# FNet mixing with a gated GLU on one core: the first tile of x cut in halves and shared by three DFT chunks

## The chip, the core and the metric

The program runs on one core of one Trainium2 chip. The core has five engines with a queue each: TensorE (matrix multiply, PE in the profile; its weight loads are PEld), VectorE (DVE), ScalarE (ACT), GpSimd (POOL) and SyncE (SP), which here only issues loads from device memory. An engine works through its own queue in order; a semaphore holds an instruction until what it reads has been written. The metric is the device time of one execution in microseconds (us), median of several runs; lower is better.

## The reference, cut to what matters

```python
x = A_x                                  # [1, 2048, 512], float32
xn = _layernorm(x, axis=-1)              # (x - mean) / sqrt(var + 1e-5)
a = einsum("bsd,ed->bse", xn, dft_hid_re)
b = einsum("bsd,ed->bse", xn, dft_hid_im)
s = einsum("ts,bse->bte", dft_seq_re, a) - einsum("ts,bse->bte", dft_seq_im, b)
g = silu(einsum("bsf,fd->bsd", sigmoid(xn @ w_gate) * (xn @ w_up), w_down))
return x + s * g
```

The sequence has 2048 rows, the hidden width is 512, the GLU's inner width 1792. The DFT matrices and weights are inputs like any other.

## The kernel before, in words

All matrix products are made in a fast 32-bit form that rounds its operands. To keep the accuracy each operand is cut into a high part (the rounded value) and a low part (value minus high part), and each product is made of three matmuls: high by high, low by high, high by low (`mm3`, line 68). The high part is a copy on ScalarE that rounds as it writes (L120, L375), the low part a subtraction on VectorE (L125, L378). The products are arranged in Strassen's manner (seven products for eight), which is why sums of blocks are made on the way.

The program is one list of **units**, written out by hand in order. A unit is a small group of matmuls. Before unit n is issued, loads for the units up to n + 5 are issued, operands of the units up to n + 2 are cut in parts, and functions hung on n run: `sooner(n, ...)` before that cutting, `amid(n, ...)` after it and before the unit's matmuls, `after(n, ...)` behind them. As each engine works in order, this list sets the order on every queue.

The first stage is the DFT along the sequence. x lies in four row tiles for each half j of the sequence, `xs[j, pp]`, each of 2 x 512 columns on 128 partitions (index e = 0, 1 for the two rows that a partition holds). The DFT matrix comes in chunks t of 512 columns; the first three chunks run together (`TOGETHER = 3`). Units 0, 1, 2 are tile 0 of x with chunks 0, 1, 2; units 3, 4, 5 are tile 1; units 6, 7, 8 are tile 2; units 9 to 11 tile 3. Each such unit has 12 matmuls (two column blocks d, two halves e, three part products). The weights of the matmul are the parts of normalised x, the moving operand the parts of the chunk.

A tile of x needs its layer norm first. `stats` (L165) runs on VectorE the statistics of a row (L178) and their aggregate (L179) and adds epsilon (L171); GpSimd makes minus the mean (L172), the power -1/2 (L173) and the bias (L174). ScalarE then writes the normalised high part, and normalises x in place (`normed`, L372); VectorE makes the low part (L378). For the first tile `begin` does this by hand with every load, high part and low part in its place; `settle` (L449) normalises x in place on VectorE. While nothing has landed, TensorE runs 13 matmuls on a tile of ones, whose results are not used.

For tile 1, `begin` makes parts too. For tiles 2 and 3 `begin_seq` hangs them on the units: statistics four units ahead, high part of the chunk and `prepare` two units ahead.

Tile pages of 4 KB on each partition come from one pool of 54; loads go down SyncE's queue in program order.

Of the kernel before, what the change touches and what calls it, by code (L numbers as in the profile page):

```python
# [8 lines left out]
F32 = mybir.dt.float32  # L9
# [23 lines left out]
def fnet_glu_kernel(ctx: ExitStack, tc: tile.TileContext, x, x_t, c_re, c_im, w_h, w_gu, w_down, out):  # L33
# [14 lines left out]

    ones = const.tile([P, 512], F32R, name="ones")
    nc.vector.memset(ones.bitcast(F32), 1.0)  # L50
# [103 lines left out]
    def fetch(j, pp):  # L154
        xs[j, pp] = page([2, D], F32)
        if (j, pp) == (0, 0):
            for e in range(2):
                nc.sync.dma_start(xs[j, pp][:, e, :], halves(x[pp, j])[:, e, :])
        else:
            nc.sync.dma_start(xs[j, pp], x[pp, j])  # L160

    def moment(pp, m, j):
        return moments[:, pp, m, j, :]

    def stats(j, pp, apart=False):  # L165
        mv = stat.tile([P, 2, 2], F32, name="mv")
        rs = stat.tile([P, 2], F32, name="rs")

        def scale(e):
            mean, by, bias = (moment(pp, m, j)[:, e] for m in range(3))  # L170
            nc.vector.tensor_scalar(rs[:, e], mv[:, e, 1], EPS, None, op0=ALU.add)  # L171
            nc.gpsimd.tensor_tensor(mean, mv[:, e, 0], minus[:, e], op=ALU.mult)  # L172
            nc.gpsimd.tensor_tensor(by, rs[:, e], mhalf[:, e], op=ALU.pow)  # L173
            nc.gpsimd.tensor_tensor(bias, mean, by, op=ALU.mult)  # L174

        for e in range(2):
            st = stat.tile([P, 6], F32, name="st")
            nc.vector.bn_stats(st, xs[j, pp][:, e, :])  # L178
            nc.vector.bn_aggr(mv[:, e, :], st)  # L179
# [44 lines left out]

    def c_block(t, pp, j, m):
        v = (c_re, c_im)[m][j, pp, t]
        return Load(halves(v) if t < 2 and pp == j == m == 0 else v, [2, SB])

    class Sum(Value):
# [22 lines left out]

    TOGETHER = 3
    CHAIN = {1: "a", 6: "a", 7: "a", 4: "a", 2: "b", 5: "c", 3: "c"}

    class Chunk:
# [33 lines left out]

        def run(self, k, pp):
            ch = "p" if k < 3 and self.t < TOGETHER else CHAIN[k]
            if k in (1, 5) and pp == 0:
# [85 lines left out]

    def prepare(pp):  # L380
        parts, src = tile_of(pp)
        for e in range(2):
            normed(pp, parts[0], src, e)
        for e in range(2):
            normed(pp, src, src, e)
        return parts, src

    def begin_seq():
        tags = {"p": "a", "c": "pd", "a": "a"}, {"p": "b", "c": "b", "a": "c"}, {"p": "c", "c": "pd", "a": "a"}, {"a": "c", "b": "a", "c": "pd"}
        chunks = [Chunk(t, tags[t], t in (1, 2)) for t in range(NT)]  # L390
        for i, k in enumerate((1, 2)):
            for pp in range(4):
                for c in chunks[:TOGETHER]:
                    add(c.needs(k, pp), lambda c=c, k=k, pp=pp: c.run(k, pp))
                m = TOGETHER * (4 * i + pp)
# [4 lines left out]
                else:  # L400
                    if pp > 1:
                        sooner(m - 4, lambda pp=pp: stats(0, pp, True))
                        sooner(m - 2, units[m][0][1].high)
                        sooner(m - 2, lambda pp=pp: ready.append(prepare(pp)))
                        for e in range(2):
                            amid(m - 2, lambda e=e: low(*ready[-1], e))
                    if pp > 2:
# [18 lines left out]
    def begin(chunks):  # L426
        for i, tag in enumerate(("gb", "ub", "pd", "pd")):
            idle = bank(tag)
            for _ in range((4, 4, 3, 2)[i]):
                nc.tensor.matmul(idle, ones[:, :P], ones, start=True, stop=True)  # L430
        first, second = (chunks[t].op[1, 0] for t in range(2))
        fetch(0, 0)
        for c in (first, second):
            c.raw = c.loads[0].at = page([2, SB], F32)
            c.parts = page([2, SB]), page([2, SB])
            for e in range(2):
                nc.sync.dma_start(c.raw[:, e, :], c.loads[0].src[:, e, :])
        fetch(0, 1)
        for n in (2, 3):
            units[n][0][1].load()  # L440
        fetch(0, 2)
        for n in (4, 5):
            units[n][0][1].load()
        mv = stats(0, 0, True)
        a, src = tile_of(0)

        def settle(e):
            v = src[:, e]
            nc.vector.tensor_scalar(v, v, mv[:, e, 0:1], moment(0, 1, 0)[:, e : e + 1], op0=SUB, op1=ALU.mult)  # L449

        normed(0, a[0], src, 0)
        for e in range(2):
            high(first.parts, first.raw, e)
        settle(0)
        low(a, src, 0)
        settle(1)
        high(a, src, 1)
        for e in range(2):
            low(first.parts, first.raw, e)
        low(a, src, 1)  # L460
        first.at = first.parts
        for e in range(2):
            high(second.parts, second.raw, e)
        second.get()
        units[2][0][1].high()
        stats(0, 1, True)
        a, src = tile_of(1)
        normed(1, a[0], src, 0)
        normed(1, src, src, 0)
        units[2][0][1].get()  # L470
        low(a, src, 0)
        units[3][0][1].high()
        normed(1, a[0], src, 1)
        normed(1, src, src, 1)
        units[3][0][1].get()
        low(a, src, 1)

# [479 lines left out]
def _layout(inputs):  # L957
# [25 lines left out]
    c_re = seq(inputs["A_dft_seq_re"])  # L983
    apart([x[0, 0], c_re[0, 0, 0], c_re[0, 0, 1]])
    return {
# [26 lines left out]
```

## Time and profile before

| | |
|---|---|
| median of 3 runs | 793.86 us (793.84 to 794.58) |
| the profiled execution | 793.51 us, of which the span of the profile is 791.7 us |
| granted TensorE clock in that execution | 0.999 of full speed |
| TensorE matmuls | 3469, busy 786.4 us |
| VectorE, ScalarE, GpSimd busy | 670.9, 518.9, 142.6 us |
| moved by DMA | 182.07 MB, mean 230 GB/s |
| DMA from 8 to 40 us of the span | above 400 GB/s, busy throughout |

A row of the timeline has the start in us, the length in us, engine, line of the kernel, operation, what is written and read, shape, how often in a row, and in brackets how long the engine had been idle before and what ended that. Instructions of one engine overlap a little at their ends, so the distance of two starts is shorter than a length. A row of a group has line, engine, operation, names and shapes, count, then busy us and mean ns of one, then idle time before them. A row of loads has destination and source, queue, count, size of one, and us from issue to landing. SPq is SyncE's queue.

### The profile page before, as it was taken

Reading aid. Unit: us, or ns where it says so; the run is one execution under the profiler, and the core shown is the slowest. Engines: PE = TensorE matmul, PEld = TensorE weight load, DVE = VectorE, ACT = ScalarE, POOL = GpSimd, SP = SyncE. Lnnn points to the kernel's source line nnn. Section 1 sums busy time; section 2 is a strip of 40 time slices with the busy share of each in tenths; the row PEclk is TensorE's granted clock in tenths of the full one; section 3 lists DMA queues with packets and bytes.
Section 4 is the critical chain, followed back from the end, with each engine's and each line's share of the span. In section 5 each row is a group of like instructions: output and inputs, shape, how many; then the busy total and the mean of one; then the engine's idle time right before and its main releaser. Section 6 shows DMA issues by size and latency. Waiting matters only on the chain.

```text
span 791.7 us, 9921 instructions
## 1 busy us (share of the span) xinstructions
PE 786.4 (99%) x3469; PEld 650.8 (82%) x3469; DVE 670.9 (85%) x879; ACT 518.9 (66%) x791; POOL 142.6 (18%) x198
## 2 busy tenths in 40 slices
PE   9999999999999999999999999999999999999998
PEld 7888888888888888888888888888888888888886
DVE  7887999788869798899999888668869898896967
ACT  6995755535434546677887867576577787887571
POOL 4452000000111002012111131122222111111301
PEclk9999999999999999999999999999999999999999
DMA  9949673385797246849965996799999898999996
GB/s 345 408 145 304 153 266 134 134 317 198 253 336 223 106 144 219 236 176 213 207 127 96 222 243 171 225 206 292 299 291 258 185 230 218 231 288 304 268 352 175
DMA packets 53186, 182.07 MB, mean 230 GB/s; under 512 B 5904, under 2 KB 6160, under 8 KB 53136
## 3 DMA queue, kind: packets, MB, share of 16 engines
q0 software_dynamic: 23360, 77.62, 44.4%
q1 hardware_dynamic: 29776, 103.82, 35.9%
q8 instruction: 27, 0.44, 0.2%
q14 instruction: 23, 0.19, 0.1%
HBM read 114.29 MB, written 70.27 MB: 233 GB/s over the span
## 4 chain that ended last, share of the span: by engine, by line
PE 99%; DMA 0%; DVE 0%; ACT 0%; POOL 0%; issue 0%; POOLq 0%
PE pd L72 28%; PE ga L72 17%; PE ua L72 17%; PE uc L72 12%; PE gc L72 12%; PE gb L72 7%; PE ub L72 7%; DMA page<-in_x_dram 0%; DVE st L178 0%; ACT page L372 0%; POOL moments L173 0%; ACT page L375 0%; DVE page L880 0%; DVE page L881 0%; POOL moments L174 0%
## 5 line engine op out<-in xcount | busy, mean ns | idle before, releaser
L125 DVE TENSOR_TENSOR page<-page 128x1024 fp32r<-128x1024 f32 (+1 forms) x381 | 346.6, 940 | 70.9 <-ACT page L120 69.2
L120 ACT ACTIVATE page<-page 128x512 fp32r<-128x512 f32 (+1 forms) x380 | 299.6, 830 | 113.7 <-DVE page L129 92.0
L72 PE MATMUL pd<-page 128*128 128x512 f32 (+1 forms) x972 | 236.9, 388 | 0.0
L72 PEld LDWEIGHTS pd<-page 128*128 128x128 f32 x972 | 182.0, 188 | 37.5
L129 DVE TENSOR_TENSOR page<-page 128x1024 f32<-128x1024 f32 (+2 forms) x244 | 195.4, 820 | 0.9
L72 PE MATMUL ga<-page 128*128 128x512 f32 x600 | 157.0, 389 | 0.2 <-ACT page L375 0.2
L72 PE MATMUL ua<-page 128*128 128x512 f32 x600 | 156.8, 389 | 0.0
L72 PEld LDWEIGHTS ga<-page 128*128 128x128 f32 x600 | 112.6, 188 | 24.4 <-ACT page L375 1.0
L72 PEld LDWEIGHTS ua<-page 128*128 128x128 f32 x600 | 112.6, 188 | 23.3
L556 POOL DMA_DIRECT2D g_part<-page x76 | 65.3, 859 | 266.4 <-ACT page L565 150.9
L72 PE MATMUL gc<-page 128*128 128x512 f32 x408 | 106.6, 389 | 0.0
L72 PE MATMUL uc<-page 128*128 128x512 f32 x408 | 106.6, 389 | 0.0
L565 ACT ACTIVATE page<-pd 128x512 f32<-128x512 f32 x140 | 82.4, 598 | 24.7 <-PE pd L72 17.4
L72 PEld LDWEIGHTS uc<-page 128*128 128x128 f32 x408 | 76.6, 188 | 15.9
L72 PEld LDWEIGHTS gc<-page 128*128 128x128 f32 x408 | 76.6, 188 | 15.9
L72 PE MATMUL gb<-page 128*128 128x512 f32 (+1 forms) x240 | 62.4, 383 | 0.0
L72 PE MATMUL ub<-page 128*128 128x512 f32 x228 | 60.9, 389 | 0.0
L72 PEld LDWEIGHTS gb<-page 128*128 128x128 f32 x240 | 44.2, 188 | 8.9
L72 PEld LDWEIGHTS ub<-page 128*128 128x128 f32 x228 | 42.8, 188 | 8.9
L314 POOL DMA_DIRECT2D f_raw<-page x16 | 8.8, 548 | 195.7 <-DVE page L326 134.8
L673 ACT ACTIVATE page<-ga 128x512 f32<-128x512 f32 x28 | 16.6, 593 | 17.9 <-PE ga L72 15.9
L691 DVE TENSOR_TENSOR page<-page 128x512 f32<-128x512 f32 x28 | 19.3, 689 | 10.0 <-ACT page L688 9.3
(101 smaller groups left out, 381.8 us busy)
## 6 DMA issues: line engine op xcount, KB each, us to landing
g_part<-page POOLq DMA_DIRECT2D x84, 512.0 KB, 7.2
page<-in_c_re_dram SPq DMA_DIRECT2D x46, 512.0 KB, 7.8
page<-in_c_im_dram SPq DMA_DIRECT2D x32, 512.0 KB, 6.8
page<-f_raw SPq DMA_DIRECT2D x28, 512.0 KB, 7.6
page<-in_w_gu_dram SPq DMA_DIRECT2D x22, 512.0 KB, 6.0
f_raw<-page POOLq DMA_DIRECT2D x16, 512.0 KB, 5.8
f_sum<-page POOLq DMA_DIRECT2D x16, 512.0 KB, 7.3
page<-f_sum SPq DMA_DIRECT2D x16, 512.0 KB, 10.2
```

Of the source, the lines that this page charges most:

```text
L72: nc.tensor.matmul(ps, ws[w], ms[m], start=first and i == 0, stop=last and i == 2, skip_group_check=go_on)
L120: nc.scalar.activation(self.parts[0], self.raw, AF.Copy)
L125: nc.vector.tensor_tensor(lo, self.raw, hi.bitcast(F32), op=SUB)
L129: (engine or nc.vector).tensor_tensor(dst, a, b, op=op)
L314: nc.gpsimd.dma_start(f_raw[self.t][block], v)
L556: nc.gpsimd.dma_start(g_part[i], pg, accum_op=ADD)
L565: nc.scalar.activation(pg[:, o, :], po, AF.Copy, scale=float(sign))
L673: nc.scalar.activation(s[k][:, m, :], ps[c + "a"], AF.Copy)
L691: nc.vector.tensor_mul(s[k][:, 0, :], s[k][:, 0, :], ps["u" + tag] if tag else s[k][:, 1, :])
```

## The change

- **Ones.** The warming matmuls read a broadcast constant of the framework instead of a tile that VectorE fills; there are 10 (3, 3, 2, 2) instead of 13.
- **Loads.** In host memory the first half (e = 0) of the first tile of x is laid out in two pieces of 256 columns, and the first block of the third chunk is laid out by halves like those of the first two. `begin` loads the two pieces, the first half of all three chunks, the second half of x, and the second halves of the three chunks; then tile 1 of x, the block of unit 3, and on as before.
- **Order of the matmuls of tile 0.** All three chunks are done with half e = 0 first, then with e = 1; units 0 to 2 hold two such groups of six matmuls each. In chunk 0 the order in a group is high by high, high x by low chunk, low x by high chunk.
- **First tile.** Statistics of the first half are taken in two pieces and aggregated. The high part of x is written by VectorE straight from x (`turned`); ScalarE normalises x in place. The low part of chunk 1's first half is made by GpSimd (`low_pool`).
- **Epsilon.** In every `stats` GpSimd adds epsilon (a constant tile `tiny`), in place of VectorE's operation; the order on GpSimd is epsilon, power, mean, bias.
- **Second tile (tile 1 of x).** Its statistics are interleaved with the low parts of the second halves of chunks 1 and 2 (`between`); the low part of unit 3's block is made in halves.
- **Units 3 to 9.** Unit 3, the fourth, takes its matmuls in another order. The statistics of tile 2 move from before the cutting of unit 4's operands to behind it (`amid`). For tiles 2 and 3 `prepare` handles one half at a time: half 0 and its low part, then the chunk's high part, then half 1.

```diff
-    ones = const.tile([P, 512], F32R, name="ones")
-    nc.vector.memset(ones.bitcast(F32), 1.0)
+    ones = nc.const_aps.tensor(1.0, [P, 512], F32).bitcast(F32R)
...
+    tiny = const.tile([P, 2], F32, name="tiny")
+    nc.gpsimd.memset(tiny, EPS)
...
-    def stats(j, pp, apart=False):
+    def stats(j, pp, apart=False, between=None):
...
-            nc.vector.tensor_scalar(rs[:, e], mv[:, e, 1], EPS, None, op0=ALU.add)
+            nc.gpsimd.tensor_tensor(rs[:, e], mv[:, e, 1], tiny[:, e], op=ADD)
+            nc.gpsimd.tensor_tensor(by, rs[:, e], mhalf[:, e], op=ALU.pow)
             nc.gpsimd.tensor_tensor(mean, mv[:, e, 0], minus[:, e], op=ALU.mult)
-            nc.gpsimd.tensor_tensor(by, rs[:, e], mhalf[:, e], op=ALU.pow)
             nc.gpsimd.tensor_tensor(bias, mean, by, op=ALU.mult)
...
             if apart:
                 scale(slice(e, e + 1))
+            if between:
+                between(e)
...
+    FIRST = {(t, e): (0, 1, 2) for t in range(TOGETHER) for e in range(2)} | {(0, 0): (0, 2, 1), (0, 1): (0, 2, 1)}
...
-                if (self.t, k, pp) == (0, 1, 0):
-                    order = (0, 0), (0, 1), (1, 0), (0, 2), (1, 2), (1, 1)
+                if part is not None:
+                    turns = [(d, part, (i,)) for i in FIRST[self.t, part] for d in range(2)]
+                elif (self.t, k, pp) == (0, 1, 1):
+                    order = (0, 0), (0, 2), (0, 1), (1, 0), (1, 2), (1, 1)
...
-    def prepare(pp):
-        parts, src = tile_of(pp)
-        for e in range(2):
-            normed(pp, parts[0], src, e)
-        for e in range(2):
-            normed(pp, src, src, e)
-        return parts, src
+    def prepare(pp, e):
+        parts, src = ready[-1]
+        normed(pp, parts[0], src, e)
+        normed(pp, src, src, e)
...
+                    if (k, pp) == (1, 0):
+                        turns = [(chunks[t], e) for e in range(2) for t in range(TOGETHER)][2 * c.t : 2 * c.t + 2]
+                        add(c.needs(k, pp), lambda turns=turns: [v.run(1, 0, e) for v, e in turns])
...
-                        sooner(m - 4, lambda pp=pp: stats(0, pp, True))
+                        (amid if pp == 2 else sooner)(m - 4, lambda pp=pp: stats(0, pp, True))
+                        sooner(m - 2, lambda pp=pp: ready.append(tile_of(pp)))
+                        sooner(m - 2, lambda pp=pp: prepare(pp, 0))
+                        sooner(m - 2, lambda: low(*ready[-1], 0))
                         sooner(m - 2, units[m][0][1].high)
-                        sooner(m - 2, lambda pp=pp: ready.append(prepare(pp)))
-                        for e in range(2):
-                            amid(m - 2, lambda e=e: low(*ready[-1], e))
+                        sooner(m - 2, lambda pp=pp: prepare(pp, 1))
+                        amid(m - 2, lambda: low(*ready[-1], 1))
...
-            for _ in range((4, 4, 3, 2)[i]):
+            for _ in range((3, 3, 2, 2)[i]):
...
+        def turned(e):
+            nc.vector.tensor_scalar(a[0][:, e], src[:, e], mv[:, e, 0:1], by[:, e : e + 1], op0=SUB, op1=ALU.mult)
+
+        def low_pool(c, e):
+            nc.gpsimd.tensor_tensor(c.parts[1][:, e], c.raw[:, e], c.parts[0][:, e].bitcast(F32), op=SUB)
+
+        sums(0)
+        turned(0)
+        high(cs[0].parts, cs[0].raw, 0)
+        normed(0, src, src, 0)
+        low(cs[0].parts, cs[0].raw, 0)
         low(a, src, 0)
+        high(cs[1].parts, cs[1].raw, 0)
+        low_pool(cs[1], 0)
+        sums(1)
+        high(cs[2].parts, cs[2].raw, 0)
+        low(cs[2].parts, cs[2].raw, 0)
+        turned(1)
+        high(cs[0].parts, cs[0].raw, 1)
+        normed(0, src, src, 1)
+        low(cs[0].parts, cs[0].raw, 1)
         low(a, src, 1)
+        high(cs[1].parts, cs[1].raw, 1)
+        high(cs[2].parts, cs[2].raw, 1)
+        third = units[3][0][1]
+        third.high()
+        stats(0, 1, True, lambda e: low(cs[1 + e].parts, cs[1 + e].raw, 1))
+        b, second = tile_of(1)
+        normed(1, b[0], second, 0)
+        normed(1, second, second, 0)
+        low(third.parts, third.raw, 0)
+        low(b, second, 0)
+        normed(1, b[0], second, 1)
+        normed(1, second, second, 1)
+        low(third.parts, third.raw, 1)
+        low(b, second, 1)
```

`sums(e)` in the new `begin` is the row statistics of half e (in two pieces for e = 0), their aggregate, and GpSimd's four operations in the new order.

More of the change, by code (lines that the diff above doesn't have):

```diff
@@ L460, in begin @@
-        low(a, src, 1)
[L461 to L476, printed above, removed]
+        mv = stat.tile([P, 2, 2], F32, name="mv")
@@ new lines, in begin, with sums @@
+        rs = stat.tile([P, 2], F32, name="rs")
+        mean, by, bias = (moment(0, m, 0) for m in range(3))
+        def sums(e):
+            parts = 2 - e
+            st = stat.tile([P, 2, 6], F32, name="st")[:, :parts]
+            for c in range(parts):
+                nc.vector.bn_stats(st[:, c], raw[:, e, c * D // parts : (c + 1) * D // parts])
+            nc.vector.bn_aggr(mv[:, e, :], st)
+            h = slice(e, e + 1)
+            nc.gpsimd.tensor_tensor(rs[:, h], mv[:, h, 1], tiny[:, h], op=ADD)
+            nc.gpsimd.tensor_tensor(by[:, h], rs[:, h], mhalf[:, h], op=ALU.pow)
+            nc.gpsimd.tensor_tensor(mean[:, h], mv[:, h, 0], minus[:, h], op=ALU.mult)
+            nc.gpsimd.tensor_tensor(bias[:, h], mean[:, h], by[:, h], op=ALU.mult)
@@ L479, in fnet_glu_kernel @@
+        normed(1, second, second, 0)
[5 more added lines that the diff above has]
+        low(b, second, 1)
+        third.at = third.parts
     XK = {(0, 0): 1, (1, 0): 2, (0, 1): 0, (1, 1): 3}
```

54 lines of the change are left out of this document (23 added, 31 removed).

## The prediction

> **What bounds the kernel now.** I read the busy table and the chain that ended last first.
>
> ```profile
> span 791.7 us, 9921 instructions
> PE 786.4 (99%) x3469; PEld 650.8 (82%) x3469; DVE 670.9 (85%) x879; ACT 518.9 (66%) x791; POOL 142.6 (18%) x198
> PE 99%; DMA 0%; DVE 0%; ACT 0%; POOL 0%; issue 0%; POOLq 0%
> ```
>
> TensorE sets the time and almost nothing else stands on the chain. All that the change can win lies ahead of the first matmul that counts, and all that it can lose is TensorE waiting later. Next I read the chain in order of time over the first 12 us, and who TensorE waited for in the whole run, the warming matmuls aside.
>
> ```profile
> 0.74 2.48 DMA page<-in_x_dram
> ...
> 5.34 0.60 ACT page L372
> 5.94 0.53 ACT page L375
> ...
> 6.52 0.50 PE ga L72
> ```
>
> ```profile
> PE ga L72 <- ACT page L375: 0.2, 1, 0.2
> ```
>
> The first real matmul starts at 6.52, after x has landed, its statistics, two ScalarE passes. TensorE's own timeline gives the pace from there.
>
> ```profile
> 1.46 2.07 PE L430 MATMUL gb<-ones 128*128 128x512 f32 x4 [1.46 <-DVE ones L50]
> 9.64 0.40 PE L72 MATMUL gb<-page 128*128 128x512 f32 x1
> 23.25 0.39 PE L72 MATMUL ga<-page 128*128 128x512 f32 x1
> ```
>
> Unit 1 starts at 9.64 and unit 6 (third tile, first chunk) at 23.25: five units of 12 matmuls, 13.61 / 60 = 0.2268 us each, without a gap. Unit 0 took 9.64 - 6.52 = 3.12 where 12 x 0.2268 = 2.72 would do, so 0.40 is lost in it. What matters for the end is when unit 6 starts and whether anything is late after it.
>
> **The start.** These rows date the loads: transfer size and issue-to-landing time, each with its issue on the queue.
>
> ```profile
> page<-in_x_dram SPq DMA_DIRECT2D x1, 256.0 KB, 3.3
> 1.18 0.42 SPq L158 DMA_DIRECT2D page<-in_x_dram  x1
> ...
> page<-in_c_re_dram SPq DMA_DIRECT2D x1, 256.0 KB, 4.1
> 1.65 0.42 SPq L437 DMA_DIRECT2D page<-in_c_re_dram  x1
> ...
> page<-in_c_re_dram SPq DMA_DIRECT2D x1, 256.0 KB, 4.5
> 2.59 0.43 SPq L437 DMA_DIRECT2D page<-in_c_re_dram  x1
> ...
> page<-in_c_re_dram SPq DMA_DIRECT2D x1, 512.0 KB, 6.8
> 4.01 0.43 SPq L81 DMA_DIRECT2D page<-in_c_re_dram  x1
> ```
>
> One 256 KB load had landed at 0.74 + 2.48 = 3.22, two at 1.18 + 3.3 = 4.48, three at 1.65 + 4.1 = 5.75, five at 2.59 + 4.5 = 7.1; after 2.6 MB in all (four 256 KB loads of c, two of x, then 512 KB of x and of c) it is 4.01 + 6.8 = 10.8. I take landings by the bytes ahead of them, since all go down one queue. So in the new order the two pieces of x's first half are there at about 2.9 and 3.3 (between 3.2 and 3.66, the latter if the second issue, 0.44 later, shifts it whole), chunk 0's first half at 4.5, chunk 1's at 5.75, x's second half at 7.1, and tile 2 of x, now behind all of the third chunk too, at 10.8.
>
> The durations are these: VectorE's forms in the first 32 us and its rows around two aggregates, ScalarE's 512-column pass, then GpSimd's rows and its one-element and two-element products.
>
> ```profile
> L178 DVE BATCH_NORM_STATS2 st<-page 128x6 f32<-128x512 f32 x10 | 6.8, 684 | 2.0 <-DMA page<-in_x_dram 1.8
> L378 DVE TENSOR_TENSOR page<-page 128x256 fp32r<-128x256 f32 x8 | 3.3, 420 | 0.4 <-ACT page L372 0.2
> L378 DVE TENSOR_TENSOR page<-page 128x512 fp32r<-128x512 f32 x2 | 1.3, 684 | 0.0
> L449 DVE TENSOR_SCALAR page<-page,mv,moments 128x256 f32<-128x256 f32 x2 | 0.8, 411 | 0.4 <-ACT page L372 0.4
> ```
>
> ```profile
> 8.79 1.23 DVE L125 TENSOR_TENSOR page<-page 128x1024 fp32r<-128x1024 f32 x1
> 9.94 0.69 DVE L178 BATCH_NORM_STATS2 st<-page 128x6 f32<-128x512 f32 x1
> 10.66 0.18 DVE L179 BATCH_NORM_AGGREGATE mv<-st 128x2 f32<-128x6 f32 x1
> ...
> 11.96 1.23 DVE L125 TENSOR_TENSOR page<-page 128x1024 fp32r<-128x1024 f32 x1
> ...
> 28.21 0.18 DVE L179 BATCH_NORM_AGGREGATE mv<-st 128x2 f32<-128x6 f32 x1
> 28.31 0.66 DVE L178 BATCH_NORM_STATS2 st<-page 128x6 f32<-128x512 f32 x1
> ```
>
> ```profile
> L375 ACT ACTIVATE page<-page 128x512 fp32r<-128x512 f32 x4 | 2.5, 624 | 0.0
> ```
>
> ```profile
> 4.47 0.57 POOL L173 TENSOR_TENSOR moments<-rs,mhalf 128x1 f32<-128x1 f32 x1
> ...
> 10.92 0.19 POOL L172 TENSOR_TENSOR moments<-mv,minus 128x1 f32<-128x1 f32 x1 [4.40 <-DVE mv L179]
> ...
> 12.12 1.48 POOL L173 TENSOR_TENSOR moments<-rs,mhalf 128x1 f32<-128x1 f32 x1
> ...
> 19.40 0.70 POOL L174 TENSOR_TENSOR moments<-moments 128x1 f32<-128x1 f32 x1
> ```
>
> ```profile
> L172 POOL TENSOR_TENSOR moments<-mv,minus 128x1 f32<-128x1 f32 x8 | 1.5, 190 | 14.9 <-DVE mv L179 14.9
> L172 POOL TENSOR_TENSOR moments<-mv,minus 128x2 f32<-128x2 f32 x4 | 0.8, 196 | 15.0 <-DVE mv L179 15.0
> ```
>
> Statistics over 256 columns have no row; they lie between an aggregate (0.18) and the 512-column row (0.68), and I take the 256-column 0.42. New chain: second piece 3.3, statistics to 3.8, aggregate to 4.0, GpSimd's epsilon (an addition like L172, 0.19) from 4.08, power 0.57 to 4.92, VectorE writes the high part straight from x (0.41) to 5.36, first matmul 5.40. Chunk 0's high part is ready by 4.5 + 0.62 = 5.1 and covers nothing. That is 1.12 sooner than 6.52, and with unit 0's 0.40 the start can win 1.5 at most. Dropping the memset of ones and three warming matmuls costs nothing there: ten at the 0.43 us of the first rows (4 matmuls, 1.46 to 3.33 where the next group starts at about that pace) fill 0.8 to 5.1. That a broadcast column feeds TensorE as fast as a written tile has no row: free, or at worst twice 0.43, ending near 9.4; I take free, the pace of every matmul row here.
>
> In the first tile VectorE runs low parts (0.68 for 512 columns, 0.42 for 256) close behind TensorE: following both queues in program order I get waits of 0.15, 0.04, 0.13, 0.15, 0.04, 0.11, 0.07, together 0.69, so unit 3 could start at 5.40 + 36 x 0.2268 + 0.69 = 14.25.
>
> GpSimd's **low part** of 512 columns has no row. Below it lies VectorE's 0.68 for the form; above, 0.19 plus 511 times the 6 ns by which two elements cost more than one, 3.3. I take 1.3, twice VectorE's row, as it is the same form. It runs from 6.6 (chunk 1's half landed at 5.75, high part 6.54); the matmul needs it at 7.86, and the end feels it only from about 1.6 on, since x's second half (7.1 + 0.7 + 0.2) keeps the next step late anyway.
> The Trainium skill (GPSIMD Engine Reference, Elementwise — side-by-side cycle accounting) gives about 2.6 cycles an element at 1.2 GHz for such an operation; worked out, an estimate of 1.1 us. The sum would be the same by it; by 3.3 us it would not, and no row here decides.
>
> **The second tile: where I see it given back.** The long GpSimd rows are the key. The power takes 0.57 at 4.47 and 1.48 at 12.12; a product takes 0.19 at 10.92 and 0.70 at 19.40. What differs is VectorE. A GpSimd operation that starts inside a two-input VectorE operation ends only after it (12.12 + 1.48 = 13.60 behind 11.96 + 1.23 = 13.19). Before, the first half's three operations fitted between the aggregate at 10.66 and the low part at 11.96, 1.30 later, thanks also to VectorE's own epsilon. Now GpSimd has four in a row and VectorE a low part between the halves. GpSimd starts 0.08 after an aggregate ends (10.92 after 10.84), VectorE's next operation already 0.10 after it began (28.31 after 28.21).
> The Trainium skill (SBUF — State Buffer, 🔬 SBUF: two separate sides) calls the port pair that the two share an exclusive lock, held by whichever starts first; then GpSimd's low part would also stop VectorE. No row shows that direction; it changes the sum only if that part lasts past 7.95, where chunk 2's low part is due, and belongs to the slow rival below.
>
> Call S the start of tile 2's statistics: 10.83 (landing 10.8; VectorE is free of tile 1's last low part then, too). Aggregate to S+0.90; the low part of chunk 1 runs S+0.82 to S+1.50, so the epsilon ends at S+1.54, power S+2.19, mean S+2.38, bias under the next low part, S+2.97. Second half: epsilon under the fourth unit's low part, S+3.58, power S+4.23, mean and bias under two more, S+5.20. Without any meeting the second bias would be there at S+3.71.
>
> ```profile
> 14.05 1.22 ACT L372 ACTIVATE page<-page,moments 128x256 fp32r<-128x256 f32 x2
> 15.18 1.04 ACT L120 ACTIVATE page<-page 128x1024 fp32r<-128x1024 f32 x1
> 19.78 1.06 ACT L120 ACTIVATE page<-page 128x1024 fp32r<-128x1024 f32 x1 [1.63 <-DMA page<-in_c_re_dram]
> 20.75 2.06 ACT L372 ACTIVATE page<-page,moments 128x256 fp32r<-128x256 f32 x4
> ```
>
> Passes over a half follow each other by about 0.5 (2.06 for four). ScalarE before: tile 2's second half at 14.05, unit 4's high part 15.18 to 16.22. Now the first half is normalised from 13.83 (unit 3 starts 14.47), the second from 16.07, unit 4's high part ends at 16.07 + 1.02 + 1.05 = 18.14. Queued behind it are the statistics of tile 3, which moved behind unit 4's low part on VectorE (18.17, next operation 1.15 later, as 9.94 behind 8.79): aggregate done at 20.22, epsilon and power to 21.14, then the mean meets unit 5's low part (20.96 to 22.19), bias at 22.50. Two passes over the half, then unit 6's high part 23.55 to 24.60. TensorE, released at 18.18 for unit 4, would be ready at 23.62 and waits to 24.64. Its load, landed at 19.78 now, is no longer what counts. Against 23.25 that is **+1.39**. Followed on in the same way, unit 9's high part is done at 32.3 and the unit starts at 33.0, so nothing is added, and I carry it to the end.
>
> The other edits cost nothing: three more loads issue at 0.43 each while the queue is ahead of the transfers; the fourth unit's low part in halves (2 x 0.68 for 1.23) is counted above.
>
> Sum: the profiled execution took 793.51 (span 791.7 and 1.81 around it), so 794.9; the median of the runs shown is 793.86, 0.35 above, and 793.86 + 1.39 = **795.2**.
>
> **The rivals.** *The meetings fall out.* They hang on margins of 0.17 (epsilon behind the aggregate) and 0.18 (mean behind the power). Without them unit 6 follows at 22.4 to 22.7, -0.6 to -0.9: 793.1; with only one of them, about 794.2. For it: tiny timing shifts suffice. Against: every GpSimd row that starts inside such a VectorE operation is long. *No stall at all* wins 1.5, 792.4, and more only if x lands before 2.9. *GpSimd's low part is the bound:* slower. Each us beyond 1.6 goes through the epsilon queued behind it to tile 1's second half; at 3.3 it adds 1.7: 796.9. For it: the 6 ns per element; against: those are too short to tell a slope from a fixed cost. *The edit does not bring the first matmul forward* (ScalarE gets chunk 0's half no sooner than now, 5.94): then 6.5 again, nothing won, and unit 6 is late by the same chain, 795.2.
>
> **How the numbers follow.** About 0.2% (1.59 us) is what a measurement can tell from no change, and the forecast sits just inside it. Forecast 0.50, its own range 794.6 to 796.0 (0.3 us for landings, and 0.24 for tile 3's last low part in unit 6, which I left out): 0.28 of it within 0.2%, 0.22 slower; no earlier first matmul 0.05, divided 0.03 and 0.02. Meetings fall out, wholly or in part, 0.30, within but for 0.05 faster; no stall 0.05, 0.03 of it faster; low part as bound 0.10, slower. Faster 0.08, within 0.58, slower 0.34. Range 792.9 to 796.2: the low end nearly reaches the case without stall, the high end the slow rival at 2.6 us.
>
> **What would show it.** First real matmul near 5.4; low part on GpSimd 0.7 to 1.6; tile 2's statistics at 10.8; GpSimd rows of 0.5 to 1.1 there; TensorE waits at the starts of units 3 and 6, the latter for ScalarE. Wrong, if unit 6 starts before 23.25 or if TensorE waits for weights in unit 1.

## The result, and the profile after

| | before | after |
|---|---|---|
| median of 13 runs each on one chip | 793.84 us (793.56 to 794.58) | 795.75 us (795.12 to 796.44) |
| profiled execution (span) | 793.51 us (791.7) | 795.81 us (794.0) |

The ratio is 1.0023, 95% interval 1.0014 to 1.0031: slower, as the interval leaves out 1; whether by more than the 0.2% that the prediction counts as telling stays open, as 1.002 lies inside it. The prediction was 795.2 in a range of 792.9 to 796.2. One execution of experiment 5 below ran at a granted clock of 0.557 and took 1335.06 us; the range given there is that of its other ten.

The first lines of the page after: span, busy times, and shares of the chain that ended last.

```profile
span 794.0 us, 9927 instructions
...
PE 788.4 (99%) x3466; PEld 649.2 (82%) x3466; DVE 668.2 (84%) x869; ACT 519.5 (65%) x792; POOL 145.5 (18%) x212
...
PE 96%; POOL 1%; DVE 1%; DMA 1%; ACT 1%; SPq 0%; issue 0%
```

GpSimd has 14 instructions more and VectorE 10 fewer. TensorE's share of the chain fell from 99% to 96%: other engines now stand on it, GpSimd among them. TensorE's waits after (engine, tile and line, who was waited for: total us, times, longest) say where.

```profile
PE ga L73 <- ACT page L121: 0.8, 1, 0.8
...
PE ga L73 <- DVE page L473: 0.6, 1, 0.6
```

The wait that before was 0.2 us at the first matmul is 0.6, on VectorE's high part of x now, and there is a new one of 0.8. Waits of the weight loads are not in this list; they show in the distances of the matmuls. The tiles of x are counted from 0 here, as in the kernel; the prediction counts them from 1, so that its tile 2 is tile 1 here. TensorE's timeline after places the two waits: the first real matmul, the second half of tile 0, the starts of units 3, 4 and 6, the second half inside unit 6, then units 7, 13, 14 and 15.

```profile
5.94 0.47 PE L73 MATMUL ga<-page 128*128 128x512 f32 x1 [0.56 <-DVE page L473]
...
10.48 0.47 PE L73 MATMUL ga<-page 128*128 128x512 f32 x1
...
15.04 0.50 PE L73 MATMUL ga<-page 128*128 128x512 f32 x1
...
18.48 0.66 PE L73 MATMUL gb<-page 128*128 128x512 f32 x2
...
24.93 0.50 PE L73 MATMUL ga<-page 128*128 128x512 f32 x1 [0.79 <-ACT page L121]
...
26.53 0.50 PE L73 MATMUL ga<-page 128*128 128x512 f32 x1
...
28.03 0.61 PE L73 MATMUL gb<-page 128*128 128x512 f32 x2
...
44.35 0.61 PE L73 MATMUL gb<-page 128*128 128x512 f32 x2
...
47.26 0.73 PE L73 MATMUL gc<-page 128*128 128x512 f32 x2
...
50.14 0.62 PE L73 MATMUL ga<-page 128*128 128x512 f32 x2
```

At the pace of 0.2268 us a matmul, 36 matmuls take 8.16 and a unit of 12 takes 2.72. What is lost in each stretch is the distance of the starts less that:

| us | prediction | after |
|---|---|---|
| first real matmul, against 6.52 | 5.40: -1.12 | 5.94: -0.58 |
| lost from there to unit 3 | 0.69 + 0.22 = 0.91 | 15.04 - 5.94 - 8.16 = 0.94 |
| lost in unit 3 and before unit 4 | 18.18 - 14.47 - 2.72 = 0.99 | 18.48 - 15.04 - 2.72 = 0.72 |
| lost in units 4, 5 and before unit 6 | 24.64 - 18.18 - 5.44 = 1.02 | 24.93 - 18.48 - 5.44 = 1.01 |
| lost inside unit 6 | left out | 28.03 - 24.93 - 2.72 = 0.38 |
| later: unit 14 | 0 | 50.14 - 44.35 - 5.44 = 0.35 |
| no longer lost: unit 0 of before | -0.40 | -0.40 |
| sum | +1.40 | +2.42 |

The spans differ by 794.0 - 791.7 = 2.3, the last column less 0.1 that comes back behind. The medians are only 1.91 apart, because the profiled execution of before lies 0.33 below its median and that of after 0.06 above. By unit 3 nothing is left of the earlier start: it begins at 15.04, and at 15.09 in the kernel before.

The chain that makes unit 6 late, in the changed kernel: VectorE's rows for the second and third tile of x, then GpSimd's.

```profile
11.40 0.69 DVE L175 BATCH_NORM_STATS2 st<-page 128x6 f32<-128x512 f32 x1
12.12 0.18 DVE L176 BATCH_NORM_AGGREGATE mv<-st 128x2 f32<-128x6 f32 x1
12.22 0.67 DVE L381 TENSOR_TENSOR page<-page 128x512 fp32r<-128x512 f32 x1
12.81 0.69 DVE L175 BATCH_NORM_STATS2 st<-page 128x6 f32<-128x512 f32 x1
...
20.24 0.18 DVE L176 BATCH_NORM_AGGREGATE mv<-st 128x2 f32<-128x6 f32 x1
...
21.14 1.21 DVE L126 TENSOR_TENSOR page<-page 128x1024 fp32r<-128x1024 f32 x1
```

```profile
12.38 0.56 POOL L168 TENSOR_TENSOR rs<-mv,tiny 128x1 f32<-128x1 f32 x1 [1.99 <-DVE mv L176]
13.02 0.55 POOL L169 TENSOR_TENSOR moments<-rs,mhalf 128x1 f32<-128x1 f32 x1
...
20.51 0.19 POOL L168 TENSOR_TENSOR rs<-mv,tiny 128x1 f32<-128x1 f32 x1 [4.38 <-DVE mv L176]
...
21.29 1.10 POOL L170 TENSOR_TENSOR moments<-mv,minus 128x1 f32<-128x1 f32 x1
22.47 0.19 POOL L171 TENSOR_TENSOR moments<-moments 128x1 f32<-128x1 f32 x1
```

The epsilon at 12.38 takes 0.56 where an addition alone takes 0.19 (the same line at 20.51): it began inside the low part of 12.22 to 12.89. The power at 13.02, under statistics, takes its usual 0.55: these statistics did not hold it up. The mean at 21.29 began 0.15 after unit 5's low part and ended at 22.39, behind its end at 22.35. ScalarE stood idle for that bias.

```profile
22.70 1.24 ACT L375 ACTIVATE page<-page,moments 128x256 fp32r<-128x256 f32 x2 [2.41 <-POOL moments L171]
23.84 1.04 ACT L121 ACTIVATE page<-page 128x1024 fp32r<-128x1024 f32 x1
```

Unit 6's high part ends at 24.88 and TensorE starts at 24.93, each step as the prediction chained it, 0.2 to 0.3 us later.

### The profile page after: what moved, and what is told of

It reads as the page before. It is cut to its first block, busy times and chain, and to the rows that moved or that the text cites. A ratio compares the mean times of both kernels' runs of the same rounds, so it can differ in the third digit from the quotient of the medians.

```text
span 794.0 us, 9927 instructions
## 1 busy us (share of the span) xinstructions
PE 788.4 (99%) x3466; PEld 649.2 (82%) x3466; DVE 668.2 (84%) x869; ACT 519.5 (65%) x792; POOL 145.5 (18%) x212
## 4 chain that ended last, share of the span: by engine, by line
PE 96%; POOL 1%; DVE 1%; DMA 1%; ACT 1%; SPq 0%; issue 0%
PE pd L73 28%; PE ga L73 17%; PE ua L73 17%; PE gc L73 11%; PE uc L73 11%; PE gb L73 6%; PE ub L73 6%; DMA page<-in_x_dram 1%; ACT page L375 0%; ACT page L121 0%; POOL moments L169 0%; POOL moments L170 0%; POOL rs L168 0%; SPq L449 0%; DVE st L175 0%
## 5 line engine op out<-in xcount | busy, mean ns | idle before, releaser
L126 DVE TENSOR_TENSOR page<-page 128x512 fp32r<-128x512 f32 (+1 forms) x378 | 343.1, 939 | 71.2 <-ACT page L121 68.0
L121 ACT ACTIVATE page<-page 128x1024 fp32r<-128x1024 f32 (+1 forms) x379 | 298.7, 830 | 112.8 <-DVE page L130 92.8
L723 DVE TENSOR_TENSOR page<-page 128x512 f32<-128x512 f32 x28 | 19.3, 690 | 10.3 <-ACT page L720 9.7
```

What stands on the lines that cost most here:

```text
L121: nc.scalar.activation(self.parts[0], self.raw, AF.Copy)
L126: nc.vector.tensor_tensor(lo, self.raw, hi.bitcast(F32), op=SUB)
L723: nc.vector.tensor_mul(s[k][:, 0, :], s[k][:, 0, :], ps["u" + tag] if tag else s[k][:, 1, :])
```

## The experiments

Theory A, the prediction's: the time goes where GpSimd's row of four operations meets VectorE's two-input low parts. It has two halves: a fourth operation in the row, and VectorE's slot for epsilon, now empty, so that its next low part starts sooner. The rivals: B, the order of the loads, which brings tile 1 of x late; C, the places of the statistics (tile 2's behind unit 4's low part, tile 1's interleaved with low parts) or of unit 6's high part; D, the low part on GpSimd.

**1. Epsilon back on VectorE**, all else as changed (the first tile keeps its own sums).

```diff
-            nc.gpsimd.tensor_tensor(rs[:, e], mv[:, e, 1], tiny[:, e], op=ADD)
-            nc.gpsimd.tensor_tensor(by, rs[:, e], mhalf[:, e], op=ALU.pow)
+            nc.vector.tensor_scalar(rs[:, e], mv[:, e, 1], EPS, None, op0=ALU.add)
             nc.gpsimd.tensor_tensor(mean, mv[:, e, 0], minus[:, e], op=ALU.mult)
+            nc.gpsimd.tensor_tensor(by, rs[:, e], mhalf[:, e], op=ALU.pow)
```

> The changed kernel, but in the statistics of tiles 1 to 3 of x (and of the second half of the sequence) VectorE adds epsilon again and GpSimd keeps three operations; the first tile stays as changed. Theory A (the fourth GpSimd operation and the VectorE operation that it freed let GpSimd meet VectorE's two-input low parts): in tile 2 the mean and bias of the first half no longer meet unit 5's low part, unit 6 starts near 23.3 instead of 24.93, unit 7 near 26.0 instead of 28.03, and the time falls by about 2 us to 793.7. Theory B (the new load order, tile 1 of x behind three chunks, sets the delay): tile 2's statistics stay where they are and unit 6 stays late; the time falls by less than 0.3 us. Theory C (the statistics of tile 2 were put too late): likewise less than 0.3 us.

Measured 793.64 us (792.98 to 794.56), ratio to before 0.9998 (0.9989 to 1.0007). All of the slowdown is gone with this edit. It also puts the mean back ahead of the power, where it runs beside VectorE's epsilon; what that order is worth alone was not run. GpSimd's row for tile 2's first half, with VectorE's low part of unit 5 below it, in this kernel:

```profile
19.47 0.19 POOL L169 TENSOR_TENSOR moments<-mv,minus 128x1 f32<-128x1 f32 x1 [4.38 <-DVE mv L176]
19.66 0.55 POOL L170 TENSOR_TENSOR moments<-rs,mhalf 128x1 f32<-128x1 f32 x1
20.28 0.19 POOL L171 TENSOR_TENSOR moments<-moments 128x1 f32<-128x1 f32 x1
20.47 0.19 POOL L169 TENSOR_TENSOR moments<-mv,minus 128x1 f32<-128x1 f32 x1
20.66 1.48 POOL L170 TENSOR_TENSOR moments<-rs,mhalf 128x1 f32<-128x1 f32 x1
```

```profile
20.51 1.23 DVE L126 TENSOR_TENSOR page<-page 128x1024 fp32r<-128x1024 f32 x1
```

The first half's bias is done at 20.47, 0.04 before the low part; of tile 2 only the second half's power is held (1.48), and nobody waits for it. Units 3, 4 and 6 start at 15.03, 17.77 and 23.21: the same start of unit 3 as in the changed kernel, and no loss beyond it. So with that loss gone the change is worth nothing that can be measured.

**2. The statistics of tile 2 in their old place**, ahead of unit 4's low part; all else as changed, epsilon on GpSimd.

```diff
-                        (amid if pp == 2 else sooner)(m - 4, lambda pp=pp: stats(0, pp, True))
+                        sooner(m - 4, lambda pp=pp: stats(0, pp, True))
```

> The changed kernel, but the statistics of tile 2 stand ahead of unit 4's low part on VectorE again. Theory A: only part comes back, since the meetings in tile 1 stay (0.6 to 0.8 us, to about 795.0), with a new wait of about 0.5 in unit 4 for its low part. Theory C: all of the 2 us comes back, 793.8. Theory B: no change.

Measured 794.75 (794.42 to 796.12), ratio 1.0013 (1.0005 to 1.0022). Unit 6 starts at 24.02 instead of 24.93, with 0.43 of that there by unit 4 (18.05; 18.48) and units 4 and 5 losing 24.02 - 18.05 - 5.44 = 0.53 instead of 1.01. But mean and bias now each meet a low part, and unit 4 waits for its own, which is behind the statistics:

```profile
19.11 1.10 POOL L170 TENSOR_TENSOR moments<-mv,minus 128x1 f32<-128x1 f32 x1
20.29 1.06 POOL L171 TENSOR_TENSOR moments<-moments 128x1 f32<-128x1 f32 x1
```

The place decides how much is lost, not whether: still slower than before. The intervals of this ratio and of the changed kernel's overlap, so the size of the gain, 1.0 us by the medians, is uncertain.

**3. The low part of chunk 1 on VectorE** instead of GpSimd.

```diff
-        low_pool(cs[1], 0)
+        low(cs[1].parts, cs[1].raw, 0)
```

> The changed kernel, but the low part of chunk 1's first half is made by VectorE instead of GpSimd. Theory A: no change beyond 0.3 us, because x's second half lands later than that part is done on either engine. Rival D (the low part holds GpSimd up, and epsilon and power of the second half are late behind it): about 0.5 us faster.

Measured 795.72 (795.34 to 796.25), ratio 1.0024 (1.0015 to 1.0033): no change against 795.75. D falls for the changed kernel.

**4. The kernel before with nothing but epsilon on GpSimd**, in the new order of operations.

```diff
+    tiny = const.tile([P, 2], F32, name="tiny")
+    nc.gpsimd.memset(tiny, EPS)
...
-            nc.vector.tensor_scalar(rs[:, e], mv[:, e, 1], EPS, None, op0=ALU.add)
-            nc.gpsimd.tensor_tensor(mean, mv[:, e, 0], minus[:, e], op=ALU.mult)
+            nc.gpsimd.tensor_tensor(rs[:, e], mv[:, e, 1], tiny[:, e], op=ADD)
             nc.gpsimd.tensor_tensor(by, rs[:, e], mhalf[:, e], op=ALU.pow)
+            nc.gpsimd.tensor_tensor(mean, mv[:, e, 0], minus[:, e], op=ALU.mult)
```

> The kernel before, with nothing changed but that GpSimd adds epsilon (order epsilon, power, mean, bias). Theory A: this alone is slower by 1.0 to 1.3 us, 794.9 to 795.1: the first matmul 0.3 later, the rest by waits in units 3 and 6 for tiles 1 and 2. Theories B and C: 0.3 us at most, the longer chain of the first tile.

Measured 795.11 (794.82 to 795.19), ratio 1.0015 (1.0006 to 1.0024). Without any of the change's loads, places or low parts, the one edit costs 1.3 us. Not all of that is loss at low parts: the longer row of the first tile makes the first real matmul 0.28 later (6.80), and 0.18 more is lost up to unit 3 (15.54). Then units 3 to 4 are 18.63 - 15.54 = 3.09 apart, units 6 to 7 27.24 - 24.07 = 3.17, both instead of 2.72: 0.37 and 0.45. Units 4 and 5 lose nothing here, where the changed kernel loses 1.01. GpSimd's mean for tile 2, 0.15 behind VectorE's low part of 18.62:

```profile
18.77 1.10 POOL L175 TENSOR_TENSOR moments<-mv,minus 128x1 f32<-128x1 f32 x1
```

**5. Epsilon on VectorE, and two loads moved ahead**: x's second half ahead of chunk 2's first half, tile 1 of x ahead of chunk 2's second half.

```diff
-            if e:
-                nc.sync.dma_start(raw[:, 1, :], v[P * D :].rearrange("(p d) -> p d", p=P))
-            for c in cs:
+            for t, c in enumerate(cs):
+                if (e, t) == (0, 2):
+                    nc.sync.dma_start(raw[:, 1, :], v[P * D :].rearrange("(p d) -> p d", p=P))
+                if (e, t) == (1, 2):
+                    fetch(0, 1)
                 nc.sync.dma_start(c.raw[:, e, :], c.loads[0].src[:, e, :])
...
-        fetch(0, 1)
```

> The changed kernel with epsilon back on VectorE in the later statistics, and with x's second half loaded ahead of chunk 2's first half, tile 1 of x ahead of chunk 2's second half. Theory A with load order as the next limit: the second half's statistics and tile 1's start about 0.8 and 0.4 us sooner, unit 3 starts 0.4 sooner than with epsilon alone and nothing gives it back, 793.2 to 793.4, below both kernels. Rival: chunk 2's halves are late in place of x's, and the time stays at 793.6.

Measured 793.19 (792.99 to 793.78), ratio 0.9993 (0.9984 to 1.0002). Beside experiment 1 (793.64) the loads are worth 0.45 us by the medians (the intervals overlap): B is at most a small term and not the cause of the loss. VectorE's low part of chunk 2 takes 1.09 instead of 0.68 in this kernel, and GpSimd's low part lies under its start, one row of each engine:

```profile
7.49 1.09 DVE L381 TENSOR_TENSOR page<-page 128x512 fp32r<-128x512 f32 x1
```

```profile
6.74 1.29 POOL L477 TENSOR_TENSOR page<-page 128x512 fp32r<-128x512 f32 x1 [1.24 <-ACT page L378]
```

It began 0.54 before GpSimd ended (8.03) and lasted 0.55 past that: here GpSimd holds VectorE.

**6. GpSimd's low part behind the second half's sums** (epsilon on VectorE as in 1), to see the low part meet VectorE's in the other order. It was executed once.

```diff
-        low_pool(cs[1], 0)
         sums(1)
+        low_pool(cs[1], 0)
```

> As with epsilon back on VectorE, but GpSimd makes chunk 1's low part behind the epsilon, power, mean and bias of x's second half, at about 10.3 us, when VectorE has two-input low parts to make. The matmul that needs it waits until about 11.6 to 12.1, so the time rises by 2.5 to 3.5 us to about 796.5. What it is for: if the shared port is held by whoever starts first, VectorE's low part that falls into GpSimd's 1.3 us (or the one that starts second) is longer or later by up to 1.3; if VectorE always goes first, GpSimd's row is stretched to 1.8 or 2 and VectorE's rows keep their 0.68 and 0.42.

That execution took 797.58, TensorE waiting 3.2 us for that part. Behind the wait its granted clock was 0.73 from 13.0 to 19.3 us, with matmuls 0.43 apart from 13.24 to 16.23 instead of 0.23, so not all of the lost time is the wait. The two VectorE operations that meet the low part, then GpSimd's:

```profile
9.73 0.68 DVE L381 TENSOR_TENSOR page<-page 128x512 fp32r<-128x512 f32 x1
...
10.54 1.29 DVE L381 TENSOR_TENSOR page<-page 128x256 fp32r<-128x256 f32 x1
```

```profile
9.82 1.72 POOL L476 TENSOR_TENSOR page<-page 128x512 fp32r<-128x512 f32 x1
```

GpSimd began 0.09 after the first of them, of 512 columns, and took 1.72 instead of 1.29. VectorE's second, of 256 columns, lasted 1.29 instead of 0.42 and ended 0.29 after GpSimd's. By these rows whichever began first went through in its usual time, and the other ended only after it. D has a price of its own, but only where TensorE needs the part.

**7. Tile 1's statistics not interleaved** with the low parts of chunks 1 and 2 (epsilon on VectorE).

```diff
-        stats(0, 1, True, lambda e: low(cs[1 + e].parts, cs[1 + e].raw, 1))
+        stats(0, 1, True)
+        for c in cs[1:]:
+            low(c.parts, c.raw, 1)
```

> As with epsilon back on VectorE, but tile 1's statistics are not interleaved with the low parts of chunks 1 and 2: both halves of the statistics first, then the low parts. Theory A: GpSimd meets no low part in the first half, yet chunk 1's low part comes 0.7 to 0.9 later than its matmul wants it, so TensorE waits about 1.2 us in unit 2 and the time rises by 0.7, to 794.4. Rival (the interleaving itself is what costs): faster, 793.2.

Measured 794.01 (793.85 to 794.70), ratio 1.0004 (0.9995 to 1.0013), 0.4 above experiment 1 with overlapping intervals. TensorE waits 1.6 us for chunk 1's low part, in an execution (794.70, the highest) where tile 1 landed late. So interleaving doesn't lose time; how much it wins is open.

**8. Unit 6's high part ahead of the first half's passes**, as before the change, epsilon on GpSimd.

```diff
+                        sooner(m - 2, units[m][0][1].high)
                         sooner(m - 2, lambda pp=pp: ready.append(tile_of(pp)))
                         sooner(m - 2, lambda pp=pp: prepare(pp, 0))
                         sooner(m - 2, lambda: low(*ready[-1], 0))
-                        sooner(m - 2, units[m][0][1].high)
```

> The changed kernel, but unit 6's high part (and unit 9's) stands ahead of tile 2's normalising on ScalarE again, as before. Theory A: unit 6 starts about 1.0 sooner, at 23.9 to 24.2, but then waits some 0.6 inside for tile 2's second low part, as the bias is as late as it was; the time falls by 0.4 to 0.7, to about 795.2. Rival (the new order on ScalarE is the cause of the late unit 6): all of it comes back, 794.0 or less.

Measured 794.91 (794.38 to 795.78), ratio 1.0013 (1.0004 to 1.0022): 0.8 less than the changed kernel by the medians (the intervals overlap), and 1.1 more than before. Unit 6's start is no longer held by its own high part (24.28), but its second half waits at 26.22 for VectorE's low part of x. From unit 4 to unit 7 this kernel loses 27.71 - 18.79 - 8.16 = 0.76, the changed one 28.03 - 18.48 - 8.16 = 1.39. So more than half of the slowdown remains; the rest hangs on the new place of this high part, behind passes that wait for the late bias.

**9. The changed kernel, with an addition of epsilon on VectorE into a tile that nobody reads.** GpSimd still makes all four operations.

```diff
+            nc.vector.tensor_scalar(spare[:, e], mv[:, e, 1], EPS, None, op0=ALU.add)
             nc.gpsimd.tensor_tensor(rs[:, e], mv[:, e, 1], tiny[:, e], op=ADD)
```

> The changed kernel, and VectorE again runs an addition of epsilon in `stats`, into a tile that nobody reads; GpSimd still makes all four operations. It separates the two halves of the cause: the fourth operation in GpSimd's row, and the earlier start of VectorE's next low part. If only the fourth operation counts, nothing changes: 795.7, unit 6 at 24.9. If only VectorE's earlier start counts, all comes back: 793.7, unit 6 at 23.2. If both do, as I think: unit 4 near 17.9, unit 6 near 24.3, unit 7 near 27.3, about 794.9.

Measured 795.19 (794.76 to 796.33), ratio 1.0019 (1.0010 to 1.0028). More work on VectorE, and 0.6 less than the changed kernel by the medians (the intervals overlap). The profiled execution is the slowest of its runs, as x's second piece landed 0.4 later in it (statistics at 4.09 after 3.68); the distances can still be read:

```profile
16.05 0.39 PE L73 MATMUL ga<-page 128*128 128x512 f32 x1
...
18.79 0.63 PE L73 MATMUL gb<-page 128*128 128x512 f32 x2
...
25.37 0.50 PE L73 MATMUL ga<-page 128*128 128x512 f32 x1 [0.96 <-ACT page L121]
```

Unit 3 loses 18.79 - 16.05 - 2.72 = 0.02 instead of 0.72, but TensorE had lost more ahead of it: from the first real matmul (6.34) to unit 4 it takes 12.45, in the changed kernel 12.54. Units 4 and 5 still lose 1.14. For tile 1 the epsilon gets in ahead of the low part now (0.19 at 13.06), and the first half's bias is ready 2.55 after the statistics began (12.08) instead of 2.94; the power, under the low part, takes 0.87. For tile 2 the bias began at 21.84, 0.01 after the low part of 21.83, and took 1.26.

**10. Epsilon on VectorE, with an unused addition on GpSimd** ahead of its three operations: a fourth operation alone.

```diff
             nc.vector.tensor_scalar(rs[:, e], mv[:, e, 1], EPS, None, op0=ALU.add)
+            nc.gpsimd.tensor_tensor(spare[:, e], mv[:, e, 1], tiny[:, e], op=ADD)
             nc.gpsimd.tensor_tensor(mean, mv[:, e, 0], minus[:, e], op=ALU.mult)
```

> The kernel with epsilon back on VectorE, and GpSimd also adds epsilon into a tile that nobody reads, ahead of its three operations: the fourth operation alone, without VectorE's earlier start. If the length of GpSimd's row counts, unit 3 comes about 0.25 later than 15.03 by tile 1's bias, and 793.9 to 794.1; if tile 2's first bias, which had 0.23 to spare ahead of unit 5's low part, is caught as well, unit 6 comes near 24.1 and the time is 794.5. If only VectorE's slot counts, 793.6 as before.

Measured 795.13 (794.72 to 795.75), ratio 1.0017 (1.0008 to 1.0025): 1.5 above experiment 1, more than the 0.3 to 0.9 that I had worked out. I had looked at the first half's bias alone, which got through (21.00 to 21.19, before a low part at 21.14 could hold it). What was caught is the second half, in this kernel's rows of GpSimd and TensorE:

```profile
15.22 0.50 POOL L173 TENSOR_TENSOR moments<-moments 128x1 f32<-128x1 f32 x1
...
21.15 1.26 POOL L170 TENSOR_TENSOR spare<-mv,tiny 128x1 f32<-128x1 f32 x1
```

```profile
14.75 0.40 PE L73 MATMUL ga<-page 128*128 128x512 f32 x1
...
18.07 0.65 PE L73 MATMUL gb<-page 128*128 128x512 f32 x2
...
23.55 0.42 PE L73 MATMUL ga<-page 128*128 128x512 f32 x1
...
25.38 0.50 PE L73 MATMUL ga<-page 128*128 128x512 f32 x1 [0.25 <-DVE page L383]
...
26.88 0.62 PE L73 MATMUL gb<-page 128*128 128x512 f32 x2
```

Unit 3 loses 0.60, unit 6 0.61 in its second half, and 0.47 more is lost from unit 7 to unit 15 (49.12), against a first real matmul 0.29 earlier than in experiment 1 (5.60; 5.89). One operation of 0.19 us costs 1.5 us, for the most part through what it pushes into VectorE's low parts; the 0.47 was not followed back.

**11. The loads of experiment 5, and the first tile in the same manner**: epsilon on VectorE, chunk 1's low part on VectorE behind the sums.

```diff
-            nc.gpsimd.tensor_tensor(rs[:, h], mv[:, h, 1], tiny[:, h], op=ADD)
+            nc.vector.tensor_scalar(rs[:, h], mv[:, h, 1], EPS, None, op0=ALU.add)
...
-        low_pool(cs[1], 0)
         sums(1)
+        low(cs[1].parts, cs[1].raw, 0)
```

> The kernel with epsilon on VectorE in `stats` and the loads in the other order, and for the first tile too epsilon on VectorE, and chunk 1's first low part on VectorE behind the second half's statistics instead of on GpSimd ahead of them. If GpSimd's low part, ahead of the second half's operations in its queue, still costs something once x lands sooner, VectorE writes the second half's high part at 8.9 instead of 9.31 and the second half of tile 0 starts up to 0.36 sooner: 792.8 to 793.0. If what is lost there is VectorE's own time, unchanged: 793.2; later by the stretch of the power under a low part, 793.4.

Measured 792.75 (792.61 to 793.65), ratio 0.9989 (0.9980 to 0.9998): below both kernels, by 0.1% against before. TensorE's rows: first matmul, second half of tile 0, units 3 and 6.

```profile
5.44 0.47 PE L73 MATMUL ga<-page 128*128 128x512 f32 x1
...
10.10 0.39 PE L73 MATMUL ga<-page 128*128 128x512 f32 x1
...
14.19 0.39 PE L73 MATMUL ga<-page 128*128 128x512 f32 x1
...
22.35 0.39 PE L73 MATMUL ga<-page 128*128 128x512 f32 x1
```

From 10.10 on nothing is lost up to unit 6 (54 matmuls in 12.25 us), which starts 0.90 before that of before. I had expected the gain at the start of the second half; it came behind it, where experiment 5 lost 0.6 (10.04 to 14.75), with the second half's high part of x written at 8.59 instead of 9.31 and tile 1's statistics at 10.16 instead of 10.79. In the changed kernel the first tile has a meeting of its own, which the prediction does not name: GpSimd's epsilon for x's second half began at 8.69 inside VectorE's low part of 8.52 and took 0.56.

## Why the prediction held, and which terms were off

**The mechanism held.** Experiments 1 and 4 show it from both sides: epsilon on GpSimd in `stats` is enough for a loss in the old kernel (1.3 us, 0.82 of it in units 3 and 6), and taking it back removes all of it from the new one (2.1). Experiment 10 shows the first half of A alone, the longer row, at 1.5. The second half, VectorE's slot, is seen in the rows of experiment 9 (tile 1's first bias 0.4 sooner), but its 0.6 is not clear of noise in the times. Experiment 8 adds a condition: some 0.6 of the loss, by one profiled execution of each kernel, also needs unit 6's high part to stand behind the first half's passes, as the prediction's chain had it. The chain named for unit 6 (power free, mean under unit 5's low part, bias, two passes, high part) is the one in the trace. Of the five meetings that it put on tile 1, four are there (12.38, 13.80, 14.30 and 15.81), and the late unit 4. The margins of 0.17 and 0.18, which carried the rival in which the meetings fall out, became 0.16 (epsilon at 12.38 behind 12.22) and 0.15 (mean at 21.29 behind 21.14).

**The start was mis-sized**: 5.94 instead of 5.40, the largest miss. I let two half-size pieces of x land at 2.9 and 3.3, by the bytes ahead of them. VectorE's rows after show what they did.

```profile
2.82 0.43 DVE L464 BATCH_NORM_STATS2 st<-page 128x6 f32<-128x256 f32 x1 [2.82 <-DMA page<-in_x_dram]
3.68 0.43 DVE L464 BATCH_NORM_STATS2 st<-page 128x6 f32<-128x256 f32 x1 [0.43 <-DMA page<-in_x_dram]
4.14 0.21 DVE L465 BATCH_NORM_AGGREGATE mv<-st 128x2 f32<-128x12 f32 x1
5.38 0.41 DVE L473 TENSOR_SCALAR page<-page,mv,moments 128x256 fp32r<-128x256 f32 x1 [1.03 <-POOL moments L468]
```

The second piece lagged the first by the distance of the issues and more (3.68, against a bound of 3.66 that the prediction gave and did not take), so cutting x in pieces bought little in this execution: the first piece landed about 0.4 before a whole half had (3.22), the second about 0.45 after. From the second piece's statistics to the high part's start took 1.70 where I had 1.65, and from its end to the matmul 0.15 where I had 0.04. The start varies between executions: with the same first tile and loads, it lies between 5.57 (experiment 2) and 6.34 (experiment 9), and in experiment 1 it is held by chunk 0's high part instead, which ended at 5.83 and had been put at 5.1. x's second half (7.69 against 7.1) and tile 1 (statistics at 11.40 against 10.83) are late in the same way, yet the stretch from first matmul to unit 3 lost 0.94 against 0.91, as these waits move with the start.

**Unit 3** lost 0.72, not 0.99: the mean of tile 1's second half got through (0.19 at 15.54), where I had put it under a low part. **Units 4 and 5** lost 1.01 against 1.02.

**Unit 6 and later** were left out or set to nothing: 0.38 in unit 6, which the prediction named with 0.24 and put in its range, and 0.35 at unit 14, which it had at 0. There the weight loads waited for ScalarE (0.46 at 47.26), and the mean of the next tile had again been stretched (0.69 for 0.20); which of the two engines' delays led to it I did not follow further. These two terms and the start make up 0.54 + 0.38 + 0.35 = 1.27, less 0.27 from unit 3: the 1.0 by which the table's first sum falls short. The median is only 0.55 above the prediction, because that added its sum to a median 0.35 above the profiled execution. So the time came nearer than the working deserved: an error in unit 3 and the choice of the median made good for part of the others, and that is luck.

**The low part on GpSimd** was taken at 1.3 and took 1.29, and does not bound (experiment 3: 795.72 without it).

The Trainium skill (GPSIMD Engine Reference, Elementwise — side-by-side cycle accounting) led to an estimate of 1.1 for it; the measurement decides, 1.29.

**The other direction of the hold-up**, of which no row of before told, exists: experiments 5 and 6 show GpSimd's low part holding VectorE's (1.09 for 0.68, 1.29 for 0.42).

The Trainium skill (SBUF — State Buffer, 🔬 SBUF: two separate sides) states just this, an exclusive lock held by the operation that starts first; experiment 6 agrees with it in both directions, experiment 5 in one.

**The rivals.** No stall at all was put at 792.4; experiment 11, with the meetings out of TensorE's way and x's loads reordered, measured 792.75. The meetings falling out was put at 793.1; experiment 1, which removes those that matter, measured 793.64, 0.5 higher; its start is 0.49 later than the prediction's (5.89; 5.40).

## What to carry to other kernels

Before moving a small operation from a busy engine to an idle one, lay both queues side by side: here a 0.19 us operation on GpSimd cost 1.5 us, for the most part because it pushed what follows into VectorE's two-input operations, and a vector operation of 0.15 us ahead of the low part had left the row more room. Where a chain of small operations feeds a tile that TensorE will need, count it to the end of the last low part that it can meet, for both halves of the tile and for every tile. Cutting a load in two to start sooner should be priced with a second landing later than the bytes ahead say: in the changed kernel's profiled execution it came 0.86 behind the first, twice the distance of the issues, and in that of experiment 10 at most 0.4 behind.

## What the hardware showed that I had not expected

The prediction had counted on GpSimd being held: an operation on 128 single elements took six times as long, 1.10 for 0.19 us, when it began 0.15 us behind a two-input vector operation. New is that statistics over 512 columns, with one input, held nothing (a power of 0.55 at 13.02 beneath them). In the other direction a vector operation on 256 columns took 1.29 instead of 0.42 us behind GpSimd's.
